# Fused attention and MoE block: the out product's PSUM in tiles of its own, with new urgencies

## The chip, the cores and the metric

The kernel runs on one core of a Trainium2 chip. The metric is the device time of one execution in microseconds (us). The kernel before takes 724.87 us (median of 3 runs, 724.75 to 725.86). One execution was profiled; every duration below is from that one.

## The reference

Two steps of attention through 32 packed queries give `x`; an MLP with an unusual gate follows. With 8 batches, 8 heads, 576 tokens and head size 64:

```python
p_packed = sm_attn(p, k, v)              # 32 packed queries read all tokens
out = sm_attn(q, p_packed, p_packed)     # all tokens read the 32 packed rows
x = out.transpose(0, 2, 1, 3).reshape(4608, 512)
h = x @ w_in                             # 512 -> 2048
sp = np.maximum(h, 0.0) + np.log1p(np.exp(-np.abs(h)))
g = h * erf(sp)
return g @ w_out                         # 2048 -> 512
```

All is in float32. A matrix product of float32 values is made of three products of a rounded high part and a low part: high by high, low by high, high by low.

## The kernel before, in words

The work goes batch by batch. For a batch, the attention is folded into the first product, so that `h` comes straight from the second attention's weights (`a2h`, `a2l`) and a small product `wp` of packed values and `w_in`. `h` is made in 16 units per batch (128 of the 2048 columns each). ScalarE (ACT) or VectorE (DVE) copies it out of PSUM, ACT makes softplus and erf, DVE multiplies: that is `g`, with features on the partitions and tokens along the row.

The product with `w_out`, the out product, has two forms.

Batches 0 to 3 take the plain one (`o_unit`): four groups of 128 tokens, each in one PSUM bank of 512 columns, taken in the order 1, 2, 3, 0. A unit adds three matmuls of 512 columns to each bank. When a sum over features ends, `done` copies each bank to a tile `ob` on ACT (L1136), and the next sum begins in the same banks. Where batches change, the next batch's first unit can stand right behind. The 64 tokens left over of two batches are paired in `o_rest`, which uses bank 0.

Batches 4 to 7 take `block`: seven products of blocks in place of eight, with sums of blocks ahead of them (`s1`, `x`) and behind them. A batch has two blocks (kh = 0, 1), so there are 8 blocks of 7 steps. A step has two half-steps (g = 0, 1) of 12 matmuls of 288 columns, for which 512 KB of prepared weights `st` come from memory (`parts`), into one of six buffers. The operand of a half-step is split into `gh` (a cast) and `gl` (a difference on DVE, L1014). The steps sum into three chains: a (steps 0 and 2), b (steps 1, 3 and 5) and c (steps 4 and 6). A chain lies in two banks. It is read after each of its steps: after steps 0 and 2 by `take` (a copy, on ACT at L1058 or DVE at L1059), after the others by `plus` (an addition on DVE, L1064). A chain is read in mid-sum, so its next step must wait for the read.

All four banks are one PSUM tile, `banks` (line 343). `buf` (lines 345 to 355) hands out slices of it: one bank for a group of tokens, banks 0 and 1 or banks 2 and 3 for a chain. A block's chains a and c take one pair and b the other, and the next block swaps them (lines 1017 to 1021).

The order of the work comes from a planner in Python (`Program.order`). Every operation has an urgency (a key, in units of `h`), worked out from the numbers in `PLAN`; the planner simulates the engines and buffers and each engine takes the most urgent operation that is ready. Buffers of a tag named in "in turn" are given out in the order in which they were asked for. What comes out is one fixed order for each engine and DMA queue. The waits between engines are then added by the framework from the tiles that instructions read and write; it is there that a tile's extent counts.

Of the kernel before, what the change touches and what calls it, by code (L numbers as in the profile page):

```python
# [10 lines left out]
F32 = mybir.dt.float32  # L11
# [9 lines left out]
PLAN = {  # L21
    "lag": 7.55,
    "act": -5.38,
    "dve": 1.44,
    "copy": 1.11,
    "steady": (-16.85, -8.13, -4.92, -17.63, -6.07, 0.42, 6.11, 7.44, -17.01, 5.83, -4.83, 4.81, -2.62, 0.88),
    "second": (-11.72, -0.9, -0.63, -9.96, -1.44, -2.31, -20.03, -23.91, -47.05, -25.48, -13.77, -14.57, 17.88, -2.64),
    "third": (1.8, 8.04, 12.47, 16.82, 23.01, 32.07, 48.17, 15.88, -4.88, -6.8, -3.28, 5.84, 8.0, 9.68),
    "wp": 2.33,
    "wi": 9.96,  # L30
    "wo": 6.63,
    "conv": 2.33,
    "rest": -2.35,
    "ends": (1, 4, 7, 9, 12, 13, 16),
    "merge": (1, 1),
    "turns": (0, 8, 16),
# [1 line left out]
    "wp first": (13.13, 24.74),  # L38
    "late": 0.18,
    "first w": (5.69, 0.5, 1.51, 4.05),  # L40
    "also": {'gate': 4.54, 'h': 1.3, 'cast': 2.54, 'taken': 0.92, 'h fast': 1.36},
    "warm": (1.4, 7.0, 0.5, 1.2),
    "pad": (1.023, 0.076, 0.113),
    "first conv": (1.71, -14.72, 21.21, 28.87),
# [11 lines left out]
    "patience": (0.174, 50.5),  # L56
    "halves": 2,
    "low until": -1.91,
    "in turn": ('st', 'gh', 'gl', 'gB', 'lB', 'cb'),
    "fast": (('st', 6), ('xb', 8), ('sb', 4), ('cb', 6), ('gB', 2), ('lB', 2)),  # L60
    "from": 4,
    "gate": (2.18, 4.6, 5.53),
    "copy fast": 0.37,
    "wp fast": 0.81,
    "steady fast": (-16.26, -8.13, -4.92, -24.25, -8.19, -1.55, 3.85, 2.62, -15.59, 11.64, -1.38, 2.77, 3.63, -1.26),
    "ml": 2.5,
    "split ahead": -0.08,
    "sums ahead": 0.7,
    "last ahead": 2.92,
    "take": 0.65,  # L70
    "st lead": -0.1,
    "keep": 0.52,
    "keep parts": (36.0, 54.81),
    "gen": (36, 58.0, 3.83),
}


# [224 lines left out]
def tile_pack_attention_moe(ctx: ExitStack, tc: tile.TileContext, qT, kT, v, pT, w_in, w_out, out, rest, out_t, parts, raw):  # L302
    nc = tc.nc
    P = 128
# [18 lines left out]
    pools, first_half = {}, ExitStack()  # L323

    def open_pool(stack, name, bufs, space=None):
        kind = {"space": bass.MemoryType.PSUM} if space else {}
        pools[name] = stack.enter_context(tc.tile_pool(name=name, bufs=bufs, reuse_waits="tile", **kind))

    for name, bufs, space in (("const", 1, None), ("attn", 2, None), ("wp", 3, None), ("tmp", 2 * G, None),
                              ("ps_o", 1, 1), ("ps_h", 2, 1), ("ps_m", 1, 1)):  # L330
        open_pool(ctx, name, bufs, space)
    open_pool(first_half, "plain", 2 * NF + 1)
    TAGS = {"p": ("attn", 1), "kvq": ("attn", 6), "big": ("attn", 2), "rem": ("attn", 1), "ms": ("attn", 1),
            "m": ("attn", 2), "sm": ("attn", 2), "pt": ("attn", 3), "a2h": ("attn", 2), "a2l": ("attn", 2),
            "mx": ("attn", 1), "wph": ("wp", 3), "wpl": ("wp", 3),
            "t0": ("tmp", G), "hs": ("tmp", 2 * G), "gh": ("tmp", 3), "gl": ("tmp", 3),
            "wo": ("plain", 2 * NF + 1), "wst": ("plain", 2), "ob": ("tmp", G),
            "ps_m": ("ps_m", 1), "ps_h": ("ps_h", 2), **{t: ("fast", n) for t, n in PLAN["fast"]}}
    room = {t: n for t, (_, n) in TAGS.items()}
    plain = {(t, i) for t, (pool, n) in TAGS.items() if pool == "plain" for i in range(n)}  # L340
    room.update({f"ps_o{y}": 1 for y in range(4)})
    prog = Program(room, {t: [plain] * n for t, n in PLAN["fast"]})
    banks = pools["ps_o"].tile([P, 4, 512], F32, name="banks")

    def buf(tag, shape, name, dtype=F32):
        if isinstance(tag, tuple):
            y = int(tag[0][-1])
            return Buf(tag, name, lambda: banks[:, y:y + len(tag), :])
        if tag.startswith("ps_o"):
            y = int(tag[-1])  # L350
            return Buf(tag, name, lambda: banks[:, y, :])
        pool, bufs = TAGS[tag]
        made = Buf(tag, name, lambda: pools[pool].tile(shape, dtype, name=name, tag=tag, bufs=bufs))
        made.turn = pool == "fast"
        return made

    def fixed(shape, name, dtype=F32):
# [3 lines left out]
    last, fresh = {}, set()  # L361
# [31 lines left out]
    wi = [None] + [fixed([P, NC, FB], f"w_in{j}") for j in range(1, NFB)]  # L393
    make_identity(nc, ident.t)
    minus = buf("ob", [P, P], "minus", F32R)
    if PLAN["lows"]:
        prog.add("POOL", -99, 0.5, 0.3, lambda: line("POOL", nc.gpsimd.tensor_scalar(
# [21 lines left out]
    def load_f32(sent, key, dst, w, src, name):  # L419
        if src.dtype == F32:  # L420
            dma(sent, src.shape[1] * P * 4, lambda: nc.sync.dma_start(dst(), src), w, ())
            return
        n = src.shape[1]
        tag = EARLY[staged[0]] if staged[0] < len(EARLY) else "wst"
        staged[0] += 1
        st = buf(tag, [P, n], name, I64)
        dma(sent, n * P * 8, lambda: nc.sync.dma_start(st[:], src), (st,), ())

        def words(i):
            return lambda: st[:].bitcast(U32).rearrange("p (n two) -> p n two", two=2)[:, :, i]  # L430
        convert(key, dst, st, words(0), words(1), n, w, (st,))
# [84 lines left out]
    a2, pt, wp = {}, {}, {}  # L516
# [472 lines left out]
        if n + 1 in ends:  # L989
            gate_group(n)  # L990

    xs, turn_of, written = {}, [0], {}

    def block(n0, b, kh):

# [12 lines left out]
        def split(x, key, name):  # L1008
            th, tl = ("gh", "gl") if name[-1] == "0" else ("gB", "lB")
            hi, lo = buf(th, [P, S], f"gh{name}", F32R), buf(tl, [P, S], f"gl{name}", F32R)  # L1010
            hi.turn = lo.turn = True
            op = act(key, S, lambda: nc.scalar.copy(hi[:], x[:]), (hi,), (x,))  # L1012
            also("cast", op, "DVE", dve_us(S, True), lambda: nc.vector.tensor_copy(hi[:], x[:]))
            dve(key, S, lambda: nc.vector.tensor_tensor(lo[:], x[:], hi[:], op=ALU.subtract), (lo,), (x, hi))  # L1014
            return hi, lo

        now = turn_of[0]
        turn_of[0] = 1 - now
        tags = [(f"ps_o{2 * y}", f"ps_o{2 * y + 1}") for y in (now, 1 - now)]
        name = f"{b}_{kh}"  # L1020
        chains = [buf(tags[0], None, f"c{name}a"), buf(tags[1], None, f"c{name}b"), buf(tags[0], None, f"c{name}c")]

        final = kh == 1 and b == B - 1

# [51 lines left out]
        made = {}  # L1076
        t = step(0, 0, 0, True, lambda g, k: split(A[0, 0, g], k, f"{name}_0_{g}"))
        m1 = take(0, t)
        ahead = PLAN["sums ahead"]
# [7 lines left out]
        t = step(2, 1, 0, False, lambda g, k: split(A[1, 0, g], k, f"{name}_2_{g}"))  # L1087
# [5 lines left out]
        t = step(4, 3, 2, True, lambda g, k: split(S1[g], k, f"{name}_4_{g}"))  # L1093
# [8 lines left out]
        t = step(6, 2, 2, False, lambda g, k: split(A[0, 0, g], k, f"{name}_6_{g}"))  # L1102
# [121 lines left out]
    made = 1  # L1224
# [10 lines left out]
    for n, (b, f, first, end) in enumerate(units):  # L1235
        prepare(n)
        h_unit(n, b, f)
        close = n + 1 in ends
        if close:
            for m in range(n + 1):  # L1240
                b, f = units[m][:2]
                if (b, f // 2, 0) in xs and f % 8 == 7:
                    block(m - 7, b, f // 8)
                if (units[m][0], units[m][1]) in gs:
                    o_unit(m, *units[m])
                    if units[m][0] % 2 and units[m][1] == NF - 1:
                        o_rest(m + PLAN["lag"] + PLAN["rest"], units[m][0] // 2)

    todo = [(op.start, op.seq, op.emit, op.fresh) for op in prog.order()]
    t, slow, margin, behind = PLAN["warm"]  # L1250
# [9 lines left out]
    for op in sorted((op for op in prog.ops if op.engine == "PE"), key=lambda op: op.start):  # L1260
        if op.start <= heads[0].start:
            while t + 0.22 < op.start - margin:
                one = 0.22 if t < slow else 0.112
                n = next((n for n in (4, 2) if t + 2 * n * one < op.start - margin), 1)
# [9 lines left out]
        t = op.start + op.busy + (op.kind and 0.1)  # L1274
# [2 lines left out]
            room_h = None if got[-1].name.startswith("wp") else got[-1]  # L1277
    todo.sort(key=lambda x: x[:2])
    for _, _, emit, new in todo:
        if "fast" not in pools and any(TAGS.get(t, ("",))[0] == "fast" for x in new for t in x.tags):  # L1280
            first_half.close()
            open_pool(ctx, "fast", 1)
        fresh.update(t for x in new for t in x.tags)
        emit()

# [43 lines left out]
```

## Time and profile before

| | |
|---|---|
| Median of 3 runs | 724.87 us |
| Profiled execution, its own time | 726.12 us |
| Its span | 724.0 us |
| Mean granted clock of TensorE | 0.998 |
| PE busy | 691.1 us (95%) |
| DVE busy | 555.3 us (77%) |
| ACT busy | 546.4 us (75%) |

PE is the matrix engine, PEld its loading of weights, which runs beside the matmuls. The span runs from the first to the last instruction in the trace, 2.12 us less than the execution's own time. Matmuls are pipelined: one of 288 columns lasts 0.29 us, but the next starts 0.13 us after it, so a stop of PE is the distance of two starts less 0.13 us; the idle time in brackets is shorter than this distance, since it counts from the modelled end. A waits row says for whom an engine waited, put down to the releaser that came last. All matmuls are issued by one helper at line 403, so that they are told apart by their tiles: `banks<-gh,st` and `banks<-gl,st` belong to blocks, `banks<-woh,gh` and its like to the plain out product, `h<-...` to the first product.

### The profile page before, as it was taken

What the parts mean: (1) busy time and instruction counts of PE and PEld (TensorE: products, weight loads), DVE (VectorE), ACT (ScalarE), POOL (GpSimd) and SP (SyncE); (2) the same over time, 40 slices, a digit from 0 to 9 for tenths busy, and PEclk for the clock granted to TensorE, in tenths of its full rate; (3) what the DMA queues carried; (4) which work ended last, traced back from release to release, by engine and by line L of the source; (5) the groups of instructions that cost most, each with busy time, mean ns of one, the idle gap of its engine ahead of it and who ended that gap; (6) DMA issues with size and microseconds to landing.
All of it is one profiled execution on the core that took longest, in us unless ns stands there. A gap on an engine that the chain in (4) does not pass through costs nothing.

```text
span 724.0 us, 14638 instructions
## 1 busy us (share of the span) xinstructions
PE 691.1 (95%) x5659; PEld 587.7 (81%) x5659; DVE 555.3 (77%) x933; ACT 546.4 (75%) x870; POOL 26.4 (4%) x29
## 2 busy tenths in 40 slices
PE   8899989999999999999999999999999999999975
PEld 4457858777788787878878799898998998998874
DVE  3999988999834699437464699879997899978762
ACT  3699899988975589677669589688887787977620
POOL 0000000001001000000000000010001100010001
PEclk9999999999999999999999999999999999999999
DMA  9955985879909677433025788787878967587795
GB/s 319 379 188 142 278 256 158 274 258 296 236 17 217 186 225 228 137 103 103 21 67 169 247 281 283 275 207 220 274 261 260 204 215 218 182 231 221 244 281 107
DMA packets 89284, 153.29 MB, mean 212 GB/s; under 512 B 25216, under 2 KB 49024, under 8 KB 89216
## 3 DMA queue, kind: packets, MB, share of 16 engines
q1 hardware_dynamic: 83536, 145.11, 61.7%
q0 software_dynamic: 5232, 6.52, 7.5%
q8 instruction: 44, 0.72, 0.4%
q10 hardware_dynamic: 448, 0.74, 0.3%
q14 instruction: 24, 0.20, 0.1%
HBM read 113.02 MB, written 39.32 MB: 210 GB/s over the span
## 4 chain that ended last, share of the span: by engine, by line
PE 78%; DVE 9%; ACT 8%; DMA 3%; issue 1%; SPq 0%; DVEq 0%; ACTq 0%
PE banks L403 49%; PE h L403 21%; PE wp L403 4%; DVE cb L1064 2%; PE s L403 2%; PE p L403 1%; DVE x L934 1%; DMA w_in<-w_in 1%; DVE gl L1014 1%; ACT ob L1136 1%; DMA v<-v 1%; ACT t L929 1%; ACT t L924 1%; ACT L924 1%; PE t L687 1%
## 5 line engine op out<-in xcount | busy, mean ns | idle before, releaser
L403 PE MATMUL banks<-gh,st 128*128 128x288 f32 x896 | 197.4, 299 | 12.3 <-DVE cb L1064 6.9
L403 PEld LDWEIGHTS banks<-gh,st 128*128 128x128 f32 x896 | 148.7, 188 | 23.9 <-DVE cb L1064 12.7
L403 PE MATMUL h<-a2h,wph 128*128 128x288 f32 x512 | 153.6, 301 | 1.4 <-ACT hs L980 0.6
L403 PE MATMUL h<-a2l,wph 128*128 128x288 f32 x512 | 150.9, 295 | 0.8 <-DVE a2l L772 0.8
L403 PE MATMUL h<-a2h,wpl 128*128 128x288 f32 x512 | 150.5, 295 | 0.2 <-DVE wpl L910 0.2
L403 PE MATMUL banks<-gl,st 128*128 128x288 f32 x448 | 132.3, 295 | 0.0
L403 PEld LDWEIGHTS h<-a2h,wph 128*128 128x128 f32 x512 | 96.0, 188 | 12.0 <-ACT hs L980 2.6
L403 PE MATMUL banks<-woh,gh 128*128 128x512 f32 x248 | 100.0, 403 | 4.2 <-ACT ob L1136 4.2
L403 PEld LDWEIGHTS h<-a2l,wph 128*128 128x128 f32 x512 | 96.0, 188 | 5.8 <-DVE a2l L772 1.3
L403 PE MATMUL banks<-woh,gl 128*128 128x512 f32 x248 | 97.5, 393 | 0.0
L403 PE MATMUL banks<-wol,gh 128*128 128x512 f32 x248 | 97.0, 391 | 0.0
L403 PEld LDWEIGHTS h<-a2h,wpl 128*128 128x128 f32 x512 | 96.1, 188 | 0.4 <-DVE wpl L910 0.4
L403 PEld LDWEIGHTS banks<-gl,st 128*128 128x128 f32 x448 | 84.2, 188 | 0.0
L1014 DVE TENSOR_TENSOR gl<-x,gh 128x576 fp32r<-128x576 f32 x96 | 71.4, 753 | 11.7 <-ACT gh L1012 11.3
L1012 ACT CAST gh<-x 128x576 fp32r<-128x576 f32 x73 | 48.6, 675 | 39.7 <-PE banks L403 36.5
L944 DVE TENSOR_TENSOR gl<-hs,gh 128x576 fp32r<-128x576 f32 (+1 forms) x64 | 46.9, 734 | 24.9 <-ACT gh L943 24.5
L403 PEld LDWEIGHTS banks<-woh,gh 128*128 128x128 f32 x248 | 46.5, 187 | 21.0 <-issue 8.2
L403 PEld LDWEIGHTS banks<-wol,gh 128*128 128x128 f32 x248 | 46.6, 188 | 10.6
L980 ACT COPY hs<-h 128x288 f32<-128x288 f32 x85 | 33.6, 399 | 26.0 <-PE h L403 24.5
L403 PEld LDWEIGHTS banks<-woh,gl 128*128 128x128 f32 x248 | 46.6, 188 | 5.6
L1064 DVE TENSOR_TENSOR cb<-cb,banks 128x576 f32<-128x576 f32 x39 | 29.4, 753 | 26.9 <-PE banks L403 26.4
L934 DVE TENSOR_TENSOR hs<-t,hs 128x576 f32<-128x576 f32 x64 | 46.9, 749 | 1.9 <-ACT t L929 1.6
(319 smaller groups left out, 1150.4 us busy)
## 6 DMA issues: line engine op xcount, KB each, us to landing
st<-parts SPq DMA_DIRECT2D x112, 512.0 KB, 4.4
q<-qT SPq DMA_DIRECT2D x32, 288.0 KB, 5.5
k<-kT SPq DMA_DIRECT2D x30, 288.0 KB, 4.8
v<-v SPq DMA_DIRECT2D x32, 256.0 KB, 5.5
wos<-w_out SPq DMA_DIRECT2D x16, 512.0 KB, 4.7
wi<-w_in SPq DMA_DIRECT2D x12, 512.0 KB, 5.2
out_t<-cb SPq DMA_DIRECT2D x16, 288.0 KB, 4.5
out_t<-cb POOLq DMA_DIRECT2D x15, 288.0 KB, 5.1
```

The lines of the kernel that those rows point to most:

```text
L403: return nc.tensor.matmul(*args, **kw)
L687: return [nc.tensor.transpose(tbanks[x]()[:, (j % 2 * 2 + r) * P:(j % 2 * 2 + r + 1) * P], a[:, r, j * P:(j + 1) * P], ident[:]) for j in ...
L924: done.append(act(n + k0, S, lambda t=t, hs=hs: nc.scalar.activation(t[:], hs[:], AF.Softplus), (t,), (hs,), run="softplus", kind=int(i < ...
L929: erfs.append(act(e + k1 + i, S, lambda t=t: nc.scalar.activation(t[:], t[:], AF.Erf), (t,), (), run="erf", kind=int(i < len(group) - 1), ...
L934: dve(key, S, lambda t=t, hs=hs: nc.vector.tensor_tensor(hs[:], t[:], hs[:], op=ALU.mult), (hs,), (t,))
L944: op = dve(key + plain, width, lambda hs=hs, ghi=ghi, glo=glo, some=some: nc.vector.tensor_tensor(glo[:, some], hs[:, some], ghi[:, some], ...
L980: op = act(n + c / 2 - PLAN["copy" if b < NS else "copy fast"], n1, lambda to=to, ps=ps, t0=t0, t1=t1, n1=n1: nc.scalar.copy(to[:, t0:t1], ...
L1012: op = act(key, S, lambda: nc.scalar.copy(hi[:], x[:]), (hi,), (x,))
L1014: dve(key, S, lambda: nc.vector.tensor_tensor(lo[:], x[:], hi[:], op=ALU.subtract), (lo,), (x, hi))
L1064: dve(mk(s, 1) - PLAN["take"], S, lambda: nc.vector.tensor_tensor(two(out), two(x), to[:, :, 0:HT], op=ALU.add), (out,), (to,) if out is x ...
L1136: act(key - 1, DM, lambda: nc.scalar.copy(ob[:], src()), (ob,), (to,))
```

## The change

The tile `banks` goes. The plain product gets four tiles of one bank (`ps_o0` to `ps_o3`), in a pool that is closed where the plain product's other buffers are. The chains get a tag of their own, `chain`: two tiles of two banks, in a pool that is opened behind that point, handed out in turn. Any chain may now take either tile. In the planner the four tiles count with the buffers that must be free before the blocks' buffers exist. The numbers of `PLAN` that bear on the blocks, and a few others, are changed.

```diff
-    "rest": -2.35,
+    "rest": -2.83,
-    "also": {'gate': 4.54, 'h': 1.3, 'cast': 2.54, 'taken': 0.92, 'h fast': 1.36},
+    "also": {'gate': -0.85, 'h': 1.3, 'cast': 0.99, 'taken': -3.02, 'h fast': 0.2},
-    "in turn": ('st', 'gh', 'gl', 'gB', 'lB', 'cb'),
+    "in turn": ('st', 'gh', 'gl', 'gB', 'lB', 'cb', 'chain'),
...
-    "ml": 2.5,
-    "split ahead": -0.08,
+    "ml": 4.45,
+    "split ahead": -2.28,
...
-    "take": 0.65,
-    "st lead": -0.1,
+    "take": 4.52,
+    "st lead": 7.48,
...
     for name, bufs, space in (("const", 1, None), ("attn", 2, None), ("wp", 3, None), ("tmp", 2 * G, None),
-                              ("ps_o", 1, 1), ("ps_h", 2, 1), ("ps_m", 1, 1)):
+                              ("ps_h", 2, 1), ("ps_m", 1, 1)):
         open_pool(ctx, name, bufs, space)
     open_pool(first_half, "plain", 2 * NF + 1)
+    open_pool(first_half, "ps_o", 1, 1)
...
-            "ps_m": ("ps_m", 1), "ps_h": ("ps_h", 2), **{t: ("fast", n) for t, n in PLAN["fast"]}}
+            "ps_m": ("ps_m", 1), "ps_h": ("ps_h", 2), **{f"ps_o{y}": ("ps_o", 1) for y in range(4)},
+            "chain": ("ps_c", 2), **{t: ("fast", n) for t, n in PLAN["fast"]}}
     room = {t: n for t, (_, n) in TAGS.items()}
-    plain = {(t, i) for t, (pool, n) in TAGS.items() if pool == "plain" for i in range(n)}
-    room.update({f"ps_o{y}": 1 for y in range(4)})
-    prog = Program(room, {t: [plain] * n for t, n in PLAN["fast"]})
-    banks = pools["ps_o"].tile([P, 4, 512], F32, name="banks")
+    plain = {(t, i) for t, (pool, n) in TAGS.items() if pool in ("plain", "ps_o") for i in range(n)}
+    prog = Program(room, {t: [plain] * n for t, (pool, n) in TAGS.items() if pool in ("fast", "ps_c")})
 
     def buf(tag, shape, name, dtype=F32):
-        if isinstance(tag, tuple):
-            y = int(tag[0][-1])
-            return Buf(tag, name, lambda: banks[:, y:y + len(tag), :])
-        if tag.startswith("ps_o"):
-            y = int(tag[-1])
-            return Buf(tag, name, lambda: banks[:, y, :])
         pool, bufs = TAGS[tag]
         made = Buf(tag, name, lambda: pools[pool].tile(shape, dtype, name=name, tag=tag, bufs=bufs))
-        made.turn = pool == "fast"
+        made.turn = pool in ("fast", "ps_c")
         return made
...
-        now = turn_of[0]
-        turn_of[0] = 1 - now
-        tags = [(f"ps_o{2 * y}", f"ps_o{2 * y + 1}") for y in (now, 1 - now)]
         name = f"{b}_{kh}"
-        chains = [buf(tags[0], None, f"c{name}a"), buf(tags[1], None, f"c{name}b"), buf(tags[0], None, f"c{name}c")]
+        chains = [buf("chain", [P, 2, 512], f"c{name}{x}") for x in range(3)]
...
-        if "fast" not in pools and any(TAGS.get(t, ("",))[0] == "fast" for x in new for t in x.tags):
+        if "fast" not in pools and any(TAGS.get(t, ("",))[0] in ("fast", "ps_c") for x in new for t in x.tags):
             first_half.close()
             open_pool(ctx, "fast", 1)
+            open_pool(ctx, "ps_c", 2, 1)
```

The multiset of PE's instructions stays as it is, and so does that of the DMA issues of SyncE. ACT has one instruction less and one more table load, DVE two instructions more: a few copies and casts change between these two engines. The order changes from the first plain units on. Three places of it follow, on PE; `...` stands for the other matmuls of each half-step or unit, and for work of the first product between them.

First, a plain product's change of batch: the last unit of batch 0 (`gh0_15`) and the first unit of batch 1 behind it (`gh1_8`). Before:

```order
L403 MATMUL banks_79<-woh15_2155,gh0_15_2116 128x512
L403 MATMUL banks_79<-woh15_2155,gl0_15_2129 128x512
L403 MATMUL banks_79<-wol15_2170,gh0_15_2116 128x512
...
L403 MATMUL h1_15_1_2240<-a2h1_799,wph1_3_1890 128x288
...
L403 MATMUL banks_79<-woh8_1532,gh1_8_2175 128x512
```

And in the changed kernel:

```order
L397 MATMUL o0_8_1_1672<-woh15_2176,gh0_15_2099 128x512
L397 MATMUL o0_8_1_1672<-woh15_2176,gl0_15_2119 128x512
L397 MATMUL o0_8_1_1672<-wol15_2192,gh0_15_2099 128x512
...
L397 MATMUL o0_8_2_1741<-woh15_2176,gh0_15_2099 128x512
...
L397 MATMUL o0_8_3_1775<-woh15_2176,gh0_15_2099 128x512
...
L397 MATMUL o0_8_0_1781<-woh15_2176,gh0_15_2099 128x512
...
L397 MATMUL h1_15_1_2255<-a2h1_814,wph1_3_1929 128x288
...
L397 MATMUL o1_8_1_2269<-woh8_1551,gh1_8_2189 128x512
```

The order is the same, with half a unit of the first product (`h1_15_1`) ahead of the new batch; the tile differs: `banks_79` for all before, and one tile for each group of tokens and batch now (`o0_8_1` is group 1 of batch 0, `o1_8_1` that of batch 1).

Second, PE at the first steps of the block 5_0 (`st5_0_s_g` is the weights of step s, half-step g). Before:

```order
L403 MATMUL banks_79<-gh5_0_0_0_5642,st5_0_0_0_5639 128x288
...
L403 MATMUL banks_79<-gh5_0_0_1_5762,st5_0_0_1_5678 128x288
...
L403 MATMUL banks_79<-gh5_0_1_0_5855,st5_0_1_0_5717 128x288
...
L403 MATMUL banks_79<-gh5_0_2_0_5864,st5_0_2_0_5795 128x288
...
L403 MATMUL banks_79<-gh5_0_1_1_5900,st5_0_1_1_5753 128x288
...
L403 MATMUL banks_79<-gh5_0_2_1_5937,st5_0_2_1_5832 128x288
```

And in the changed kernel:

```order
L397 MATMUL c5_00_5947<-gh5_0_0_0_5758,st5_0_0_0_5756 128x288
...
L397 MATMUL c5_01_5978<-gh5_0_1_0_5858,st5_0_1_0_5840 128x288
...
L397 MATMUL c5_00_5947<-gh5_0_0_1_5868,st5_0_0_1_5796 128x288
...
L397 MATMUL c5_01_5978<-gh5_0_1_1_5965,st5_0_1_1_5870 128x288
...
L397 MATMUL c5_00_5947<-gh5_0_2_0_5903,st5_0_2_0_5901 128x288
...
L397 MATMUL c5_00_5947<-gh5_0_2_1_6072,st5_0_2_1_5944 128x288
```

Steps 0 and 1 now take turns by half-steps, so that the two chains' last half-steps stand side by side, and step 2 comes whole behind them.

Third, PE near the end: the second half of the block 7_0 and the start of 7_1. Before:

```order
L403 MATMUL banks_79<-gh7_0_4_1_8170,st7_0_4_1_8093 128x288
...
L403 MATMUL banks_79<-gh7_0_5_0_8126,st7_0_5_0_8124 128x288
...
L403 MATMUL banks_79<-gh7_0_6_0_8188,st7_0_6_0_8186 128x288
...
L403 MATMUL banks_79<-gh7_0_5_1_8215,st7_0_5_1_8156 128x288
...
L403 MATMUL banks_79<-gh7_0_6_1_8296,st7_0_6_1_8217 128x288
...
L403 MATMUL banks_79<-gh7_1_0_0_8259,st7_1_0_0_8257 128x288
...
L403 MATMUL banks_79<-gh7_1_1_0_8313,st7_1_1_0_8315 128x288
...
L403 MATMUL banks_79<-gh7_1_0_1_8352,st7_1_0_1_8293 128x288
...
L403 MATMUL banks_79<-gh7_1_2_0_8335,st7_1_2_0_8354 128x288
```

And in the changed kernel:

```order
L397 MATMUL c7_02_8297<-gh7_0_4_0_8133,st7_0_4_0_8131 128x288
...
L397 MATMUL c7_01_8097<-gh7_0_5_0_8147,st7_0_5_0_8189 128x288
...
L397 MATMUL c7_02_8297<-gh7_0_4_1_8236,st7_0_4_1_8145 128x288
...
L397 MATMUL c7_01_8097<-gh7_0_5_1_8318,st7_0_5_1_8225 128x288
...
L397 MATMUL c7_02_8297<-gh7_0_6_0_8268,st7_0_6_0_8266 128x288
...
L397 MATMUL c7_10_8401<-gh7_1_0_0_8338,st7_1_0_0_8334 128x288
...
L397 MATMUL c7_02_8297<-gh7_0_6_1_8371,st7_0_6_1_8312 128x288
...
L397 MATMUL c7_10_8401<-gh7_1_0_1_8393,st7_1_0_1_8355 128x288
...
L397 MATMUL c7_11_8459<-gh7_1_1_0_8376,st7_1_1_0_8373 128x288
...
L397 MATMUL c7_10_8401<-gh7_1_2_0_8418,st7_1_2_0_8416 128x288
```

The half-steps of two chains take turns here in both; in the changed kernel the first half-step of 7_1 stands between the two of step 6 of 7_0, and a half-step of another chain stands between the last of step 0 of 7_1 and the first of step 2, which followed directly before.

## Rows read from the trace of the kernel before

**Rows 1.** Page, part 1: busy time, share of the span and instructions of each engine.

```profile
PE 691.1 (95%) x5659; PEld 587.7 (81%) x5659; DVE 555.3 (77%) x933; ACT 546.4 (75%) x870; POOL 26.4 (4%) x29
```

**Rows 2.** Page, part 4: shares of the chain that ended last, by engine.

```profile
PE 78%; DVE 9%; ACT 8%; DMA 3%; issue 1%; SPq 0%; DVEq 0%; ACTq 0%
```

**Rows 3.** Windows: stretch, length, then busy time (count) of PE, PEld, DVE, ACT, POOL.

```profile
550.00:600.00 50.00, 49.74 (x427) 47.34 (x426) 44.56 (x72) 41.05 (x65) 5.03 (x4) 1.00 0.79 213
650.00:700.00 50.00, 44.32 (x320) 42.47 (x319) 39.06 (x60) 29.98 (x45) 1.22 (x1) 1.00 0.81 246
```

**Rows 4.** Waits of the weight loads: engine, tile, line, releaser; total us, times, longest.

```profile
PEld banks L403 <- DVE cb L1064: 12.7, 19, 1.1
PEld banks L403 <- ACT ob L1136: 6.5, 8, 1.2
PEld banks L403 <- ACT cb L1058: 2.3, 2, 1.3
PEld banks L403 <- DVE cb L1059: 2.1, 3, 1.5
PEld banks L403 <- ACT gh L1012: 1.7, 3, 1.1
```

**Rows 5.** Timeline of PE near the end: start, duration, instruction, [idle before <-releaser].

```profile
678.29 0.43 PE L403 MATMUL banks<-gh,st 128*128 128x288 f32 x2
...
679.88 0.29 PE L403 MATMUL banks<-gh,st 128*128 128x288 f32 x1
681.02 0.40 PE L403 MATMUL banks<-gh,st 128*128 128x288 f32 x1 [0.85 <-DVE cb L1064]
...
688.48 0.29 PE L403 MATMUL banks<-gh,st 128*128 128x288 f32 x1
689.67 0.37 PE L403 MATMUL banks<-gh,st 128*128 128x288 f32 x1 [0.89 <-ACT gh L1012]
...
694.30 0.40 PE L403 MATMUL banks<-gh,st 128*128 128x288 f32 x1 [1.22 <-DVE cb L1059]
```

**Rows 6.** Timeline of VectorE (DVE) in the same stretch.

```profile
680.21 0.76 DVE L1064 TENSOR_TENSOR cb<-cb,banks 128x576 f32<-128x576 f32 x1 [1.40 <-PE banks L403]
...
688.81 0.75 DVE L1064 TENSOR_TENSOR cb<-cb,banks 128x576 f32<-128x576 f32 x1 [1.28 <-PE banks L403]
```

**Rows 7.** Timeline of PE at a plain product's change of batch, and at a block.

```profile
177.27 0.29 PE L403 MATMUL h<-a2h,wpl 128*128 128x288 f32 x1
177.94 0.50 PE L403 MATMUL banks<-woh,gh 128*128 128x512 f32 x1 [0.37 <-ACT ob L1136]
...
449.16 0.40 PE L403 MATMUL banks<-gh,st 128*128 128x288 f32 x1 [0.74 <-DVE cb L1064]
```

**Rows 8.** Timeline of ScalarE (ACT) at two changes of batch.

```profile
95.76 1.28 ACT L924 ACT_TABLE_LOAD   x1
97.06 0.69 ACT L924 ACTIVATE t<-hs 128x576 f32<-128x576 f32 x1
...
176.81 1.07 ACT L1136 COPY ob<-banks 128x512 f32<-128x512 f32 x2 [0.27 <-PE banks L403]
```

**Rows 9.** Timeline of VectorE: the last two reads of chains before 449.16.

```profile
443.68 0.76 DVE L1064 TENSOR_TENSOR cb<-cb,banks 128x576 f32<-128x576 f32 x1 [0.49 <-PE banks L403]
...
448.36 0.75 DVE L1064 TENSOR_TENSOR cb<-cb,banks 128x576 f32<-128x576 f32 x1
```

**Rows 10.** Page, part 5: the reads of chains by L1064 (busy, mean ns, idle before).

```profile
L1064 DVE TENSOR_TENSOR cb<-cb,banks 128x576 f32<-128x576 f32 x39 | 29.4, 753 | 26.9 <-PE banks L403 26.4
```

**Rows 11.** Instructions on `banks`: duration ns min/median/max, first and last start.

```profile
L403 PE MATMUL banks<-gh,st x896: 288/295/408, 410.0 to 717.2; 128*128 128x288 f32 x180
```

**Rows 12.** Windows of 4 us near the end; last two columns: DMA share, GB/s.

```profile
688.00:692.00 4.00, 3.11 (x24) 2.90 (x24) 3.19 (x5) 1.14 (x2) 0.00 (x0) 1.00 0.98 301
692.00:696.00 4.00, 2.78 (x22) 2.54 (x21) 4.00 (x7) 1.45 (x3) 0.00 (x0) 1.00 0.98 308
```

**Rows 13.** Page, part 6: the loads of block weights: count, KB each, us to landing.

```profile
st<-parts SPq DMA_DIRECT2D x112, 512.0 KB, 4.4
```

More of the change, by code (lines that the diff above doesn't have):

```diff
@@ L58 @@
     "low until": -1.91,
-    "in turn": ('st', 'gh', 'gl', 'gB', 'lB', 'cb'),
+    "in turn": ('st', 'gh', 'gl', 'gB', 'lB', 'cb', 'chain'),
     "fast": (('st', 6), ('xb', 8), ('sb', 4), ('cb', 6), ('gB', 2), ('lB', 2)),
     "from": 4,
[L62 to L65, printed above, removed]
-    "ml": 2.5,
-    "split ahead": -0.08,
-    "sums ahead": 0.7,
-    "last ahead": 2.92,
-    "take": 0.65,
-    "st lead": -0.1,
-    "keep": 0.52,
-    "keep parts": (36.0, 54.81),
-    "gen": (36, 58.0, 3.83),
+    "gate": (-5.75, 8.86, 10.2),
+    "copy fast": -0.62,
+    "wp fast": -0.59,
+    "steady fast": (-13.34, -10.28, -8.5, -23.16, -7.74, -1.89, -5.38, 0.64, -25.43, 11.67, -3.47, 4.52, 20.9, 1.94),
+    "ml": 4.45,
+    "split ahead": -2.28,
+    "sums ahead": -0.13,
+    "last ahead": 15.67,
+    "take": 4.52,
+    "st lead": 7.48,
+    "keep": 1.09,
+    "keep parts": (54.41, 45.84),
+    "gen": (39.63, 77.98, 2.4),
 }
@@ L990, in h_unit @@
             gate_group(n)
-    xs, turn_of, written = {}, [0], {}
+    xs, written = {}, {}
     def block(n0, b, kh):
```

## The prediction

> **What bounds the kernel now.** I read the page first: PE is busy for 95% of the span [rows 1], and the chain that ended last lies on PE for 78%, with 9% on DVE and 8% on ACT [rows 2]. So a gain must come from PE's stops, or from matmuls that go; none goes here. The windows then show where PE stops: hardly in the middle of the block stage (49.74 of 50 us busy), far more near the end, where only block products are left (44.32 of 50) [rows 3]. A busy PE still hides short stops in this table, since matmuls overlap. So third come the waits of the weight loads [rows 4]: 12.7 us for DVE's additions out of `banks`, 6.5 us for ACT's copies to `ob`, 2.3 and 2.1 us for the copies of chains. Reads of the out product's PSUM are the largest thing that PE waits for.
>
> Fourth, the timelines say whether these waits are true ones. PE starts step 5's first half-step with the pair at 678.29, whose first matmul is the last of step 4; 12 matmuls later, at 679.88, it starts the half-step's last one. That gives 1.59 us for a half-step and 0.133 us for a matmul [rows 5]. Step 4's chain was thus complete at about 678.29 + 0.29 = 678.6. Its read on DVE begins only at 680.21, with DVE idle for 1.40 us before it [rows 6]: that is 0.04 us behind the end (679.88 + 0.29 = 680.17) of the *other* chain's half-step. The next half-step, which needs that read, starts at 681.02, 0.05 us behind the read's end, and PE has stopped for 1.14 - 0.13 = 1.01 us. Had the read begun at 678.6, it would have ended at 679.4 and nothing would have stopped. The same at 688.48: the read at 688.81 begins 0.04 us after a half-step that writes another chain ends, and PE starts at 689.67, 0.11 us after the read's 689.56; this row is put down to ACT's cast, so about 0.9 of the 1.7 us of that waits row belong here [rows 4 to 6].
>
> PE also waits where its own banks are free. At 449.16 it starts 0.05 us after the end of the read at 448.36; the chain pair that it begins was read for the last time at 443.68 [rows 7, 9]. At 177.94 it begins bank 1 of a new batch 0.06 us after the end of two copies (176.81 + 1.07 = 177.88), though the first copy, which is bank 1's, ended about 0.5 us earlier [rows 7, 8]. Everything goes as if all four banks were one object: a read waits for the last write to any bank, a write for the last read of any. The kernel has one PSUM tile there.
>
> **The change, part by part.** *Tiles of their own.* What is at stake is the sum of these rows: 12.7 + 2.3 + 2.1 + 1.0 (the cast's row, with the restart) = 18.1 us for chains, and 6.5 us for `ob`, together 24.6 us [rows 4]. Stops added up from start to start, as worked out above for 681.02, give 24.4 (nine near the end of about 1.0 us each, the others mostly shorter).
>
> What of this comes back? For `ob`: where a batch begins, its first bank still needs its own copy. At 176.81 two copies go one behind the other, and half a unit of the first product stands ahead of the new batch, as it does in the changed order; that stop goes whole. At the first change ACT has a table load of 1.28 us and a softplus of 0.69 us in its line [rows 8], and I leave 0.5 us there (bounds 0 and 1.28 + 0.69 = 2.0).
>
> For chains: from a half-step's last matmul to the next possible one on the same chain it takes 0.29 + 0.04 + 0.75 + 0.05 = 1.13 us [rows 5, 6]. One half-step of another chain in between gives 1.59, so 0.46 us are spare; this sets in only when DVE is late. In the changed order no chain is taken up again directly (the stop at 694.30 with 1.22 us idle was partly such a case [rows 5]), and 12 times one half-step stands between. If DVE is always in the middle of a 0.75 us instruction, it is late by 0.37 us in the mean, within the spare; sometimes two stand ahead (1.5 - 0.46 = 1.0 us late). I take 0.15 us in each of 12: 1.8 us. Bounds: 0, and 12 x 0.75 = 9.0.
>
> *Urgencies.* PE's work is the same. DVE gets two instructions more, ACT a table load more: at most 1.28 + 2 x 0.75 = 2.8 us, beside idle times of 5.4 us (DVE) and 8.9 us (ACT) in every 50 us [rows 3]; I count 0. If that cover were gone it would be 2.8. Earlier loads of `st` pass the loads of attention's inputs and the stores of `out_t` on SyncE's queue; a load lands in 4.4 us [rows 13], with six buffers, one of them in use, 5 x 1.59 = 8.0 us of half-steps cover it, and I count 0 until the very end. Other stops of PE, which the new order may lengthen or shorten, are not shown; I bound them by the cast's and the copies' rows, 2.3 us either way [rows 4], and take 0.
>
> *The loads near the end.* In 688 to 696 the DMA engines are busy for 0.98 of the time and move 301 and 308 GB/s [rows 12], with 46 matmuls in 8 us, that is 2.09 us for each 12. Without stops PE wants 524 KB in each 1.59 us, 329 GB/s. The last 15 loads with four stores of 128 x 576 values are 9.05 MB, wanted within about 26.5 us (16.6 half-steps); at 308 GB/s 8.2 MB pass: 0.9 MB or 2.9 us short, if 308 is the most. But it was reached while PE, and so the freeing of buffers, was held up. I take 1.0 us; bounds 0, and all 21 half-steps behind the last unit of the first product at the measured 2.09 us: 21 x 0.5 = 10.5.
>
> The Trainium skill ("DMA: Bandwidth & Descriptors", section "Specifications") puts the limit of memory for one core at about 358 GB/s. By that, 9.5 MB fit into 26.5 us and this term would be 0 (an estimate); the windows here never run at that demand, so no row decides it.
>
> *Sum.* 24.6 - 0.5 - 1.8 - 1.0 = 21.3 us less. The profiled execution would go from 726.12 to 704.8. That execution lies 1.25 us above the median of the runs, 724.87; taken from the median it is 703.6, and I say **704**.
>
> **The rivals.** *The loads take over.* The stops go, but the last part runs at the pace of the loads: 10.5 us instead of 1.0 come back, so 703.6 + 9.5 = 713. For it: the share of 0.98 in just the windows where PE stops most. Against it: in those windows a load is still back in 4.4 us at the median [rows 13], far below the 8.0 us that the buffers cover.
>
> *The change doesn't do what it says.* The waits are true, and merely named after the latest event: 724.9. For it: a half-step that follows on the same chain does need the read. Against it: DVE idle 1.40 us before a read whose chain was complete, and PE's start 0.05 us behind a read of another chain [rows 6, 7, 9].
>
> *Slower: reads at the head of DVE's line.* Reads get more urgent (`take` from 0.65 to 4.52), and an engine works in order: a read that is put early holds all that stands behind it, among it the `gl` of the next half-steps, until its chain is complete. Today 39 additions cost DVE 26.9 us of idle time, 0.69 us each [rows 10], and PE hardly feels it. There are 56 reads. DVE has about 5.4 us idle in 50, so 33 in the 307 us in which blocks run [rows 11]; what goes beyond is PE's. It outweighs the gain from (33 + 21.3)/56 = 0.97 us more for each read; at 1.05 it is 59 - 33 = 26 us of stops, so 703.6 + 26 = 729 or so. Against it: exact waits let reads start earlier, as the 1.40 us show.
>
> **How the numbers follow.** My forecast 0.75, with a range of its own from 700 to 710 (at the low end 24.6 and 2.3 for other stops, about 698 to 700; at the high end 1.8 + 1.0 grown to 9); loads 0.13, no effect 0.05, slower 0.05, and 0.02 for something else, as likely faster as not. A change within 0.2% (1.45 us) is what a measurement of this kernel can't tell from none. Faster 0.75 + 0.13 + 0.02 and a part of "no effect" that still saves some: 0.92; the same 0.03; slower 0.05. The range takes in the loads' case at 713: 699.5 to 714.
>
> **What would show it.** Right: the waits for `cb` and `ob` by the out product's weight loads fall from 23.6 to under 4 us; DVE's reads begin 0.04 us after their own chain's last matmul; the window 650 to 700 has PE at 48 us or more. Loads: waits for DMA `st` appear behind 680, with a DMA share near 1. Wrong: waits of the same size for `gl` or for reads, or DVE idle in front of reads while PE waits for `gl`. The forecast fails if the waits go but others of over 10 us come, or if the gain ends near the 6.5 us of `ob` alone.

## The result, and the profile after

The changed kernel takes 705.71 us (median of 4 runs, 705.06 to 706.65), the kernel before 725.02 beside it: a ratio of 0.973, 95% interval 0.972 to 0.975. The forecast was 704, the range 699.5 to 714.

The page of the changed kernel first, parts 1 (busy time) and 4 (the chain that ended last), to set beside [rows 1, 2]:

```profile
span 704.3 us, 14652 instructions
...
PE 685.3 (97%) x5659; PEld 587.3 (83%) x5659; DVE 557.1 (79%) x935; ACT 545.0 (77%) x869; POOL 26.0 (4%) x29
...
PE 78%; ACT 7%; issue 6%; DMA 5%; DVE 2%; POOL 0%; SPq 0%; POOLq 0%; DVEq 0%; ACTq 0%
```

The same matmuls are there; the span is 19.7 us shorter. In the chain that ended last DVE's share has fallen from 9% to 2%, ACT's only from 8% to 7%. "issue", which is time in which an engine waited for nothing that the profile shows, has come up to 6% and DMA to 5%. It will matter where: the last two entries of that chain are GpSimd's time ahead of its last two stores, and no longer matmuls as in the kernel before.

```profile
685.36 7.65 issue
694.25 3.92 issue
```

The waits of PE's weight loads in the changed kernel, for [rows 4] (total us, times, longest):

```profile
PEld c L397 <- DMA st<-parts: 1.6, 1, 1.6
...
PEld h L397 <- DVE wpl L875: 1.0, 1, 1.0
...
PEld c L397 <- DVE cb L1055: 0.9, 2, 0.5
...
PEld o L397 <- ACT ob L1127: 0.8, 2, 0.5
```

Waits for reads of chains have gone from 17.1 us in 24 stops to 0.9 in 2, those for `ob` from 6.5 in 8 to 0.8 in 2. A hand-over between chains near the end, on PE and then on DVE, for [rows 5, 6]:

```profile
689.01 0.29 PE L397 MATMUL c<-gl,st 128*128 128x288 f32 x1
689.14 0.43 PE L397 MATMUL c<-gh,st 128*128 128x288 f32 x2
689.41 0.30 PE L397 MATMUL c<-gl,st 128*128 128x288 f32 x1
```

```profile
689.48 0.76 DVE L1055 TENSOR_TENSOR cb<-cb,c 128x576 f32<-128x576 f32 x1 [1.72 <-PE c L397]
690.18 0.76 DVE L1008 TENSOR_TENSOR gl<-x,gh 128x576 fp32r<-128x576 f32 x1
```

The pair at 689.14 is the last matmul of one half-step and the first of the next. DVE's read starts 0.05 us after the first of the two ends (689.43), while PE goes on into another chain. Nothing stops.

Two stretches of the changed kernel, in the columns of [rows 3]:

```profile
670.00:680.00 10.00, 9.89 (x75) 9.69 (x75) 9.92 (x16) 3.37 (x6) 0.00 (x0) 1.00 0.97 359
680.00:690.00 10.00, 10.00 (x78) 10.00 (x77) 7.07 (x11) 3.85 (x6) 1.20 (x1) 1.00 1.03 347
```

PE's last matmul in the kernel before and in the changed one:

```profile
717.29 0.29 PE L403 MATMUL banks<-gl,st 128*128 128x288 f32 x1
```

```profile
695.53 0.29 PE L397 MATMUL c<-gl,st 128*128 128x288 f32 x1
```

It starts 21.8 us earlier. The span is only 19.7 us shorter. So 2.1 us are lost behind PE's work. The timeline of GpSimd (POOL) shows where, first in the kernel before:

```profile
703.14 1.20 POOL L1073 DMA_DIRECT2D out_t<-cb  x1 [47.28 <-DMA st<-parts]
711.74 1.22 POOL L1073 DMA_DIRECT2D out_t<-cb  x1 [7.39 <-DVE cb L1064]
716.89 1.20 POOL L1073 DMA_DIRECT2D out_t<-cb  x1 [3.94 <-issue]
```

and in the changed kernel:

```profile
684.16 1.20 POOL L1064 DMA_DIRECT2D out_t<-cb  x1 [35.24 <-DMA st<-parts]
693.03 1.22 POOL L1064 DMA_DIRECT2D out_t<-cb  x1 [7.67 <-issue]
698.19 1.20 POOL L1064 DMA_DIRECT2D out_t<-cb  x1 [3.94 <-issue]
```

These are the last block's three accumulating stores of 288 KB, which add to what stands in memory. In the kernel before the third went out 0.4 us before PE's last matmul, now 2.7 us after it. The sum for the third was ready at 692.66 + 0.75 = 693.4 (the last of DVE's additions for these stores, below), that for the second at 690.24 (above). They stood waiting, put down to "issue", the third for 4.8 us and the second for 2.8.

```profile
692.66 0.75 DVE L1055 TENSOR_TENSOR cb<-cb,c 128x576 f32<-128x576 f32 x1 [1.72 <-PE c L397]
```

The time from issue to landing says what for. Of the first of these stores and of the second it was, in the changed kernel:

```profile
out_t<-cb POOLq DMA_DIRECT2D x1, 288.0 KB, 8.5
out_t<-cb POOLq DMA_DIRECT2D x1, 288.0 KB, 4.8
```

The first thus landed at 692.7, and the second went out 0.3 us later; the second landed at 697.9, and the third went out 0.3 us later. The distance of two stores follows the landing, be it 8.5 or 4.8 us.

### The profile page after: what moved, and what is told of

It reads as the page before. It is cut to its first block, busy times and chain, and to the rows that moved or that the text cites. A ratio compares the mean times of both kernels' runs of the same rounds, so it can differ in the third digit from the quotient of the medians.

```text
span 704.3 us, 14652 instructions
## 1 busy us (share of the span) xinstructions
PE 685.3 (97%) x5659; PEld 587.3 (83%) x5659; DVE 557.1 (79%) x935; ACT 545.0 (77%) x869; POOL 26.0 (4%) x29
## 4 chain that ended last, share of the span: by engine, by line
PE 78%; ACT 7%; issue 6%; DMA 5%; DVE 2%; POOL 0%; SPq 0%; POOLq 0%; DVEq 0%; ACTq 0%
PE h L397 24%; PE c L397 21%; PE o L397 20%; PE wp L397 4%; PE or L397 3%; PE s L397 2%; PE p L397 2%; DMA wi<-w_in 2%; ACT t L923 1%; PE warm L397 1%; DMA w_in<-w_in 1%; ACT t L918 1%; PE t L681 1%; ACT L918 1%; ACT hs L974 1%
## 5 line engine op out<-in xcount | busy, mean ns | idle before, releaser
L397 PE MATMUL c<-gh,st 128*128 128x288 f32 x896 | 191.9, 297 | 1.5 <-DMA st<-parts 1.4
L397 PEld LDWEIGHTS c<-gh,st 128*128 128x128 f32 x896 | 147.7, 188 | 8.8 <-issue 4.1
L397 PE MATMUL c<-gl,st 128*128 128x288 f32 x448 | 132.4, 295 | 0.0
L397 PE MATMUL o<-woh,gh 128*128 128x512 f32 x248 | 99.2, 400 | 0.1
L397 PE MATMUL o<-woh,gl 128*128 128x512 f32 x248 | 97.6, 394 | 0.0
L397 PE MATMUL o<-wol,gh 128*128 128x512 f32 x248 | 97.1, 392 | 0.0
L397 PEld LDWEIGHTS c<-gl,st 128*128 128x128 f32 x448 | 84.2, 188 | 0.0
L397 PEld LDWEIGHTS o<-woh,gh 128*128 128x128 f32 x248 | 46.5, 188 | 15.6 <-issue 8.2
L397 PEld LDWEIGHTS o<-wol,gh 128*128 128x128 f32 x248 | 46.6, 188 | 10.7
L397 PEld LDWEIGHTS o<-woh,gl 128*128 128x128 f32 x248 | 46.6, 188 | 5.7
```

Source lines behind the costliest of these rows:

```text
L397: return nc.tensor.matmul(*args, **kw)
```

## The experiments

The first four kernels ran beside each other, with the kernel before at 725.32 us. The changed kernel's 705.71 is from the measurement above, where the kernel before took 725.02, so differences from it can be some tenths of a microsecond off. The theory: one tile joined the four banks, so that a read waited for writes to other banks, and a write for reads of them. The rival: the new urgencies bring the gain.

**The order of before, with tiles of its own.** The planner and all numbers stay as before; only the tiles are made otherwise:

```diff
...
-            return Buf(tag, name, lambda: banks[:, y:y + len(tag), :])
+            return Buf(tag, name, lambda: pools["ps_c"].tile([P, 2, 512], F32, name=name, tag=f"c{y}", bufs=1))
...
-            return Buf(tag, name, lambda: banks[:, y, :])
+            return Buf(tag, name, lambda: pools["ps_o"].tile([P, 512], F32, name=name, tag=tag, bufs=1))
...
```

> The order and all urgencies of the kernel before; only the PSUM tiles are those of the changed kernel (four of one bank, then two of two banks). Theory (one tile joined the banks, so that reads and writes of different banks waited for each other): the stops go as in the changed kernel, but the one chain that is taken up again directly near the end keeps about 1 us and seven with one half-step between keep little: 706 to 709 us. Rival (the new urgencies bring the gain, the tiles only allow them): 722 to 725 us.

Measured: 706.13 us (704.35 to 707.48), ratio 0.974 (0.972 to 0.975). This lies within the theory's 706 to 709, and the rival falls: with the old order the tiles alone bring 19.2 us, all of the gain that can be measured. One wait for a read of a chain is left among the weight loads:

```profile
PEld c_1a L403 <- DVE cb L1059: 1.1, 1, 1.1
```

It is the chain that the old order takes up again directly (at 694.30 in [rows 5], at 678.60 in this run): a true wait, which the new order avoids.

**The new order, with one tile.**

```diff
...
+    banks = pools["ps_all"].tile([P, 4, 512], F32, name="banks")
...
+        if pool == "ps_o":
+            made.make = lambda: banks[:, int(tag[-1]), :]
+        if pool == "ps_c":
+            made.make = lambda: banks[:, 2 * made.slot["chain"]:2 * made.slot["chain"] + 2, :]
...
```

> The order of the changed kernel, with all four banks in one tile again. Theory: the waits between banks come back at every change of chain near the end (10 to 12 us) and at changes of batch (6 us), and in the blocks before: 720 to 730 us. Rival (the urgencies bring the gain): 706 to 708 us.

Measured: 731.33 us, ratio 1.008 (1.007 to 1.010): above the kernel before, and just above the expected 720 to 730. The urgencies alone are a loss of 6 us. The waits of this kernel's weight loads:

```profile
PEld banks L402 <- DVE cb L1060: 15.3, 20, 1.6
...
PEld banks L402 <- ACT ob L1132: 7.3, 8, 1.3
...
PEld banks L402 <- ACT cb L1054: 3.9, 4, 1.0
...
PEld banks L402 <- DVE cb L1055: 2.7, 3, 1.2
```

For chains that is 21.9 us in 27 stops, where it was 17.1 in 24 before [rows 4]: what an order costs depends on whether the banks are joined.

**One tile for the plain product alone**, the chains in their own:

```diff
...
+    banks = pools["ps_o"].tile([P, 4, 512], F32, name="banks")
...
+        if pool == "ps_o":
+            made.make = lambda: banks[:, int(tag[-1]), :]
...
```

> The changed kernel, with one tile for the plain product's four banks; the chains keep tiles of their own. Theory: the 6.5 us of waits for the copies to ob come back, and the wait of 1.65 us for wpl at 109 us, which came in their place, goes: 709.5 to 712 us. Rival (what the plain product saves is lost later at another wait anyway): 705 to 707 us.

Measured: 710.54 us, ratio 0.980 (0.978 to 0.982), within the theory's 709.5 to 712. The waits for ACT's copies to `ob` are back. Of the two waits for `wpl`, the low part of `wp`, which the changed kernel has, only the later and shorter one is left:

```profile
PEld banks L401 <- ACT ob L1131: 7.3, 8, 1.2
...
PEld c L401 <- DVE cb L1059: 0.9, 2, 0.5
...
PEld h L401 <- DVE wpl L908: 0.4, 1, 0.4
```

So the plain product's tiles are worth 4.8 us. The waits for `ob` fall by 6.5 us with them (7.3 to 0.8), but in the changed kernel PE comes earlier to 109 us and waits there for `wp` (shown below).

**One tile for the chains alone**, the plain product in four:

```diff
...
+                    pair.append(pools["ps_c"].tile([P, 4, 512], F32, name="pair"))
+                return pair[0][:, 2 * made.slot["chain"]:2 * made.slot["chain"] + 2, :]
...
```

> The changed kernel, with both chain slots in one tile of four banks; the plain product keeps its four tiles. Theory: the 18 us of waits for reads of chains come back, less about 2 us that the changed kernel loses behind its last matmul: 719 to 726 us, and together with the other half's cost about the one-tile kernel's. Rival (urgencies): 706 to 708 us.

Measured: 725.35 us, ratio 1.000 (0.999 to 1.001), within the theory's 719 to 726. The chains' tiles are worth 19.6 us in this order. The two halves cost 4.83 + 19.64 = 24.5 us beside 25.6 for both at once: they add up within 1.2 us. The waits for reads of chains are those of the kernel with one tile:

```profile
PEld pair L405 <- DVE cb L1063: 15.3, 20, 1.5
...
PEld pair L405 <- ACT cb L1057: 3.9, 4, 1.0
...
PEld pair L405 <- DVE cb L1058: 2.7, 3, 1.2
```

Three more kernels ran together, on what was lost at the end (the kernel before at 725.93 us).

**The changed kernel again.**

> The changed kernel unaltered, as the mark for the other two runs here: 705 to 706.5 us by every theory.

Measured: 705.33 us, ratio 0.972 (0.971 to 0.974).

**The last accumulating stores in halves.**

```diff
...
+                if final:
+                    for d in range(2):
+                        dma(mk(s, 1) + d / 16, P * HT * 4, lambda d=d: nc.gpsimd.dma_start(
+                            dst[:, d, :], two(t)[:, d, :], accum_op=ALU.add), (), (t,), "POOL", after=[written[b, half, c]])
+                    return
...
```

> The changed kernel, with the last block's three accumulating stores of 288 KB issued as two of 144 KB each. Theory (the end is now set by these stores, and the next one of them isn't issued until the one before has landed, for want of room in their queue): halves need half the room, the third store goes out some 3 us earlier, and the end comes 1.5 to 3.5 us earlier: 702.5 to 704.5 us. Rival (GpSimd itself needs about 5 us for a store, whatever waits): twice as many issues, same or later: 705.5 to 709 us. Second rival (the plain stores of the last step set the end): 705 to 706.5 us.

Measured: 702.82 us, ratio 0.969 (0.968 to 0.970), within the theory's 702.5 to 704.5 and below what both rivals gave. GpSimd in this run (x2 stands for two halves):

```profile
683.31 1.78 POOL L1066 DMA_DIRECT2D out_t<-cb  x2 [34.35 <-ACT cb L1049]
689.79 1.78 POOL L1066 DMA_DIRECT2D out_t<-cb  x2 [4.70 <-DVE cb L1055]
693.03 0.86 POOL L1066 DMA_DIRECT2D out_t<-cb  x1 [1.46 <-DVE cb L1055]
694.06 0.86 POOL L1066 DMA_DIRECT2D out_t<-cb  x1 [0.17 <-issue]
```

A store's two halves are both out within 1.9 us (693.03 to 694.06 + 0.86): the engine doesn't need 5 us for a store, and that rival falls. The second and the third store now begin to go out 0.3 to 0.4 us after DVE's addition is done (689.48 and 692.67). The half at 689.79 took, from issue to landing:

```profile
out_t<-cb POOLq DMA_DIRECT2D x1, 144.0 KB, 4.0
```

It landed at 693.8, so the half at 693.03 went out before that: halves don't wait for the one just ahead of them. The last half, at 694.06, followed that landing by 0.3 us. Three halves are under way at once and never four, where whole stores go singly. That fits a want of room, and not an order kept among the stores.

**The last accumulating store made plain.**

```diff
-        send(5, plus(5, t1, m1, m1), 0, 1)
...
+            dma(mk(2), P * S * 4, lambda: nc.sync.dma_start(two(had1), dst1), (had1,), (), after=[written[b, 0, 1]])
+            add(mk(5) - 2, m1, m1, had1, ALU.add)
+            plus(5, t1, m1, m1)
+            dma(mk(5, 1), P * S * 4, lambda: nc.sync.dma_start(dst1, two(m1)), (), (m1,))
...
```

> The changed kernel, with the last of the accumulating stores (step 5 of the last block) replaced: the earlier half of the sum is loaded back ahead of time, added on VectorE (0.75 us more there), and the result stored plainly from SyncE. Theory (the third accumulating store at 698.19 sets the end): the end falls to the second one, issued at 693.03, and to the last plain stores: 701 to 703 us. Rival (the stores at the end are bound by bandwidth or by the last matmul, at 695.5 in both): 705 to 706.5 us.

Measured: 701.54 us (701.37 to 702.21), ratio 0.967 (0.966 to 0.968), within the theory's 701 to 703. Its last issues, on GpSimd and then on the queue of SyncE (SPq), where 693.98 is the store that was made plain:

```profile
691.99 1.22 POOL L1064 DMA_DIRECT2D out_t<-cb  x1 [7.60 <-issue]
```

```profile
693.98 0.38 SPq L1093 DMA_DIRECT2D out_t<-cb  x1
695.37 1.14 SPq L1111 DMA_DIRECT2D out_t<-cb  x2
```

In the trace of the changed kernel run again the last matmul starts at 694.03 and the span ends at 702.6, 8.6 us later; here it is 694.56 and 699.5, 4.9 us. The gain of 3.8 us is all behind PE's work. This version is faster than both kernels.

## Why the prediction was right, point by point

- *What bounds the kernel; one object of four banks.* Right, and shown by the first two runs: tiles alone 706.1, order alone 731.3.
- *24.6 us at stake.* Right in size: the waits rows fell by 23.6 - 1.7 = 21.9 us. That the two halves, undone in the new order, cost 24.5 us is no second proof. With one tile that order waits for 21.9 + 7.3 = 29.2 us, and what the changed kernel loses at 109 us and behind its last matmul (below) is partly won back there; so near a match is luck.
- *0.5 us left for `ob`, 1.8 for chains.* 0.8 and 0.9 are left. The twelve places with one half-step in between were given 0.15 us each; in the whole trace two short waits are left, so reads nearly always come in time.
- *Urgencies at nothing.* Right beside tiles of their own: 706.13 and 705.71 lie within each other's runs. With joined banks they lose 6 us, which the sum had no term for and, with the tiles apart, didn't need.
- *1.0 us for loads near the end.* Too much. Two windows before ran at 301 and 308 GB/s [rows 12], and I took that as a possible limit. The kernel before had itself moved more, early on (the last two columns are DMA share and GB/s, as in [rows 12]), and the changed kernel does near the end, while PE hardly stops:

```profile
20.00:30.00 10.00, 7.63 (x72) 4.41 (x71) 10.00 (x22) 6.28 (x11) 0.00 (x0) 1.00 1.04 400
```

```profile
674.00:682.00 8.00, 7.89 (x60) 7.69 (x59) 7.95 (x14) 2.48 (x4) 0.00 (x0) 1.00 1.04 411
```

  So 308 was no limit, and the rival of the loads falls: no wait of a weight load for `st` appears near the end. The 4.4 us to landing that spoke against it were the median of all loads of the kernel before and not of those windows, as I wrote; the changed kernel's loads took longer near the end, and still less than the 8.0 us that the buffers cover (eight of them issued in 672 to 684):

```profile
st<-parts SPq DMA_DIRECT2D x8, 512.0 KB, 5.9
```

  The Trainium skill's limit of about 358 GB/s for one core ("DMA: Bandwidth & Descriptors", "Specifications") doesn't hold for this window either, which ran at 411, and the measurement decides. By that limit the term would have been 0, which is what came, but the trace shows no such limit at work. The one wait for `st`, 1.6 us, stands at 406.9, where the blocks begin.
- *Slower by reads at the head of DVE's line.* Did not come. DVE does stand idle before reads (1.72 us at 689.48), with PE going on.
- *Missed.* Two terms of the sum were missing, both of the kind "what is late next". At 109 us PE, now earlier, waits for the high part of `wp` and then for the low one (`wph`, `wpl`):

```profile
109.22 0.40 PE L397 MATMUL h<-a2h,wph 128*128 128x288 f32 x1 [0.21 <-ACT wph L869]
109.45 0.29 PE L397 MATMUL h<-a2l,wph 128*128 128x288 f32 x1
110.48 0.40 PE L397 MATMUL h<-a2h,wpl 128*128 128x288 f32 x1 [0.73 <-DVE wpl L875]
```

  Counted from start to start, with the slower first step after each stop (0.23 us to the next start and not 0.13), that is some 1.5 us. And behind the last matmul 2.1 us are lost to the accumulating stores, whose distances I didn't look at, since PE set the end. With both the sum would have been 21.3 + 1.0 (loads) + 0.6 (hand-overs, 2.3 forecast and 1.7 left) - 1.5 - 2.1 = 19.3, and the medians differ by 19.3. So exact a match is luck: the wait for `st` at 406.9 is new as well and isn't in this sum, nor are two waits for loads from `rest`, 1.3 us together, which the kernel before had and the changed one hasn't.
- *What would show it.* The waits for `cb` and `ob` fell from 23.6 to 1.7 us, under the 4 named, and the read at 689.48 begins 0.05 us behind its own chain's last matmul. The window 650 to 700 was badly chosen: the changed kernel's PE ends inside it, at 696. Up to there it is busy but for 0.1 us, in 670 to 680.

## What to carry to other kernels

Where an engine waits for a read, see when the data that it reads were complete: a reader that sits idle with its data ready, and starts 0.04 us behind an unrelated write, waits for the tile and not for the data. Give buffers that are handed over independently tiles of their own, before tuning an order around them: here the tiles brought 19 us and the retuned order, by itself, lost 6. When the engine that sets the time gets faster, look at the last few transfers too. And before a rate is taken for a limit, look for a higher one elsewhere in the same trace.

## What the runs showed of the hardware

Loads and stores together reached 411 GB/s over 8 us (674 to 682 in the changed kernel), and 400 GB/s over 10 us in the kernel before (20 to 30); the 308 that it showed near its end was no limit.

Accumulating stores of 288 KB from GpSimd went out singly. Where the next one stood ready, it followed 0.3 us behind the landing of the one before, whether that took 8.5 or 4.8 us. Of halves of 144 KB three were under way at once; the fourth followed a landing by 0.3 us as well. GpSimd's plain stores of 256 KB to `out` did overlap (by 1.5 to 5.1 us in the changed kernel), so it isn't the size in bytes alone. That room in their queue is the reason fits all of these; the room itself was not measured.
